# Loading q with four tokens to a partition in a fused retention and wave-MLP kernel

## The chip, the cores and the metric

The kernel runs on one core of one Trainium2 chip. The metric is the device time of one execution in microseconds. A core has five engines that run their own instruction lists in order and wait for one another by semaphores: TensorE (PE, with PEld for its weight loads), VectorE (DVE), ScalarE (ACT), GpSimd (POOL) and SyncE (SP). SP, ACT and POOL issue the DMAs; in this kernel SP and ACT issue the loads of q, k and v and the stores, SP also the transposes by DMA, POOL the loads of the weights.

## What is computed

Two layers follow one another. The first is a retention recurrence over 768 tokens, 4 batches and 8 heads of 64, the second a token- and channel-mixing layer over the 512 channels:

```python
for t in range(S):                       # q, k, v: (4, 8, 768, 64), float32
    state = gamma[h] * state + outer(k[t], v[t])
    y[t] = scale * q[t] @ state
x = y with the heads side by side        # (4, 768, 512)
theta = x @ w_theta
zr, zi = x * cos(theta), x * sin(theta)
u = x + w_tok_r @ zr + w_tok_i @ zi      # mixes tokens
out = u + relu(u @ w_ch)                 # (4, 768, 512), float32
```

gamma differs from head to head. The kernel writes the powers of gamma into q and v as factors that depend on the token's position (qsc, vsc), or into the result (qx), so that the recurrence becomes masked products of blocks.

## The kernel before

**Units.** The first layer is cut into 24 units: 4 batches, 3 blocks of 256 tokens, 2 halves of the heads. Unit n has 4 heads and 256 tokens. For each unit `Lk`, `Lq` and `Lv` load a tile of 128 partitions from k, q and v: partition p holds the tokens 2p and 2p+1 of all four heads, so a head gives a run of two tokens x 64 x 4 bytes, 512 bytes, and a load is one DMA of 512 such runs, 262144 bytes. `ck`, `cq`, `cqs` and `cv` turn the tiles into bfloat16 on POOL, DVE or ACT, `cqs` and `cv` with the position factors; the k and q halves land in one tile kqb.

**A unit's work.** `Tk` and `Tq` transpose kqb on PE and `E` copies the result to kqT (from unit 12 on `Dk` does both by DMA for some units). `A` makes the scores (L346), `m` multiplies them with the mask on DVE (L355), `Y` multiplies them with v (L423). `ST` makes the unit's contribution to the state, `S0` and `S1` sum it, `SB` writes it as a block diagonal, `I` multiplies it with q (L411). `XB` or `XA` evicts the result to xT, with heads and channels on the partitions and the tokens put back into their order. `Tx` and `Ex`, or `Dx` by DMA, transpose that into x_sb.

**The second layer.** A chunk is 128 tokens; two units (the two halves of heads) give two chunks. `Hh` makes the angles (L469), `CN` their cosine and sine on ACT (L476), `z` the products (L483). `M` mixes the tokens on PE (L509), `u` adds x, `Tu` and `Eu` or `Du` transpose, `O` multiplies with w_ch (L536), `f` finishes and `SO` stores.

**The order.** Nothing is scheduled by the compiler: ORDER is one list of tokens, each naming a function, its unit or chunk, and for copies and loads the engine (p, v, a, or s for SP). Each engine gets its instructions in the order of the list, so a token's place matters for its own engine. `Z` are warm-up matmuls on a tile of zeros: seven `Z` tokens with two matmuls each stand before `Tk.0`, seven more among the first units, one at the end. They wait for the memset of zero in `const1` on DVE, which stands behind the product arg in `const2`. `const2`, `constA`, `const4` and `const5` make the positions, the logarithms of gamma, the identity and the mask on POOL; ACT computes qsc and vsc in `const3` and the eight pieces of qx in `const8` and `const9` (L233), ahead of `ck.1.a`.

**The rotation of semaphores.** DMAs that SP and ACT issue (loads, stores, transposes) take eight completion semaphores in turn, in an order close to that of the list, whichever queue issues them. The issue of a DMA waits until the DMA that had its semaphore before has landed, and holds up what stands behind it on its queue. Before the change `Lv.4` so waits for `Lq.4`, and `Lk.5` for `Lk.4`. Tiles of the loads come from two pools, 16 for k and q, 9 for v.

Of the kernel before, what the change touches and what calls it, by code (L numbers as in the profile page):

```python
# [15 lines left out]
FT = mybir.dt.float32  # L16
# [7 lines left out]
const4 Lq.1.a const9 Lk.1.s Z.39 const8 ck.0.p Tk.0 ck.1.a cqs.0.v cv.0.v Tq.0 E.0.v Lq.4.a ST.0  # L24
Lk.4.a cqs.1.p Tq.1 Lq.2.s S0.0.v SB.0.1.v A.0 Lk.2.s SB.0.0.p cv.1.p Lv.2.s S1.0 Z.15 I.0 Z.27 m.0
Tk.1 E.1.a cqs.2.v Z.34 cv.2.p Y.0 ST.1 XB.0.1.a S0.1.v S1.1 SB.1.0.a Pth Lq.3.s Z.18 XB.0.0.v Tq.2
A.1 SB.1.1.a ck.2.a I.1 m.1 Y.1 ST.2 Tk.2 const7 Z.23 XB.1.0.v Lk.3.s E.2.v XB.1.1.v A.2 ck.3.p
S0.2.v m.2 S1.2 SB.2.1.a Z.11 cqs.3.p Tq.3 Lv.3.s Tx.0 Tk.3 Z.3 ck.4.p Lv.4.s Lk.5.s Lq.5.s Lv.5.s
Lq.6.s Lk.6.s Lv.6.s Lq.7.s E.3.a SB.2.0.v I.2 Y.2 XB.2.1.a Ex.0.a cv.3.v cq.4.p Tk.4 Lq.8.s A.3
ST.3 Lk.7.s S0.3.v SB.3.0.a S1.3 Lv.7.s Lk.8.s Tx.1 Tq.4 SB.3.1.p cv.4.p m.3 Pw.1.0 XB.2.0.a Ex.1.a  # L30
I.3 Lv.8.s E.4.a ck.5.a cq.5.a Y.3 Pw.0.0 ST.4 Hh.0 S0.4.v XB.3.0.v XB.3.1.v cv.5.v CN.0.1 A.4
CN.0.0 Tq.5 Hh.1 Tk.5 SB.4.0.p SB.4.1.a Pw.0.1 Hh.2 m.4 E.5.v I.4 Y.4 ST.5 ck.6.a Tk.6 Tx.2 cq.6.a
CN.1.1 CN.1.0 XA.4.1 A.5 XA.4.0 m.5 Lq.9.s Ex.2.v S0.5.v z.0.p Tq.6 E.6.a CN.2.0 cv.6.p Hh.3
SB.5.0.v Tx.3 Tw.1.0 z.1.v SB.5.1.a Ew.1.0.v Ex.3.a CN.2.1 A.6 I.5 Y.5 ST.6 XA.5.0 z.2.v Tw.0.0
CN.3.0 Tx.4 CN.3.1 Ew.0.0.v S0.6.v XA.5.1 Ex.4.v Hh.4 CN.4.0 CN.4.1 Tw.0.1 M.0.1 Pw.1.1 z.3.v M.0.0
Tw.0.2 Pw.1.2 Ew.0.2.a SB.6.1.a Hh.5 z.4.p SB.6.0.p Lk.9.a M.0.3 ck.7.p cqs.7.p M.0.2 CN.5.1 CN.5.0
cq.8.v m.6 Ew.0.1.v Tw.1.1 Tw.1.2 Ew.1.1.v Lv.9.s M.0.4 M.1.0 Tx.5 Ew.1.2.v M.1.1 S1.6 Tk.7 M.1.4
Pch Ex.5.v z.5.v cv.7.v Tq.8 Tq.7 M.1.2 E.7.a M.0.5 I.6 Y.6 ST.7 A.7 ck.8.a u.0 S0.7.v m.7 XA.6.1
SB.7.1.a M.1.5 M.1.3 XA.6.0 Tw.1.3 M.2.5 Pw.0.2 M.2.3 u.1 S1.7 Tk.8 M.2.1 M.2.0 SB.7.0.v Ew.1.3.a
Tu.0 I.7 cv.8.v E.8.a Lk.10.s ck.10.p cv.9.p Y.7 ST.8 A.8 cqs.9.v ck.9.v M.2.4 Du.1 Eu.0.a XB.7.1.a  # L40
# [6 lines left out]
Tu.3 Eu.3.a Dx.9 SB.10.0.a cqs.12.p u.4 Hh.9 Tq.11 ck.11.v Tu.4 z.6.v Eu.4.v ck.15.v M.5.0 M.5.4
Tk.11 E.11.a SB.10.1.p cv.11.p M.5.2 M.5.3 I.10 M.5.5 M.5.1 Lq.13.a A.11 Y.10 ck.14.v ST.11 CN.9.1
CN.9.0 SO.0.a Hh.8 u.5 S0.11.v z.9.v XB.10.0.v m.11 Dk.12 Tx.8 Tq.14 O.4 Lv.13.a SB.11.0.a Lq.15.s
Lk.13.s CN.8.1 Lk.18.a XB.10.1.a CN.8.0 SB.11.1.p cv.12.p Lq.16.s I.11 Tk.14 Ex.8.v A.12 Y.11 ST.12  # L50
f.4 Lv.15.s O.3 z.8.p E.14.a XA.11.0 XA.11.1 Hh.10 S0.12.a f.3 SB.12.0.v Tx.10 Tu.5 CN.10.1 Dx.11
Ex.10.v cq.13.p Lk.16.s Lv.17.s Hh.11 SO.2.s CN.10.0 m.12 S1.12 z.10.v Tk.15 M.6.1 M.6.2 M.6.0 M.6.3
# [12 lines left out]
S0.18.v XA.17.1 XA.17.0 O.10 SO.1.a CN.14.1 S1.18 Lv.19.a CN.14.0 Dx.16 Lq.20.a f.10 Lq.22.a
SB.18.0.a Hh.17 SB.18.1.p Eu.11.v Tq.19 I.18 Tk.19 CN.17.1 O.8 Tx.17 CN.17.0 m.18 Hh.16 z.14.p
Lv.20.s Du.9 E.19.a f.8 O.11 Y.18 cv.19.p ck.20.a CN.16.1 ST.19 A.19 CN.16.0 M.12.1 Ex.17.v f.11
cq.20.p Lk.22.s Dk.20 M.12.0 S0.19.a M.13.3 M.13.2 XB.18.1.a SB.19.1.p SB.19.0.v M.13.0 z.17.v
# [15 lines left out]
M.20.4 Mh.1.1 M.20.5 u.20 O.22 Mh.1.5 uh.1 f.22 Tu.20 SO.14.a SO.19.s Eu.20.a O.21 SO.18.a Tuh.1
Euh.1 f.21 Oa.0 Oa.1 fa.0 fa.1 Oh.0 Oh.1 SO.21.a SO.22.s SO.20.s fh.0 SOh.0 fh.1 SOh.1 Z.31
# [14 lines left out]
def kernel(  # L100
# [16 lines left out]
    P = 128  # L117
# [35 lines left out]

    def load_unit(name, src, n, e):
        b, i, h = unit(n)
        t = io.tile([P, HU, 2, D], FT, name="vf" if name == "vf" else "kqf", bufs=9 if name == "vf" else 16)
        queues[e].dma_start(  # L157
            out=t.rearrange("p h a d -> p h (a d)"),
            in_=src[b, h * HU:(h + 1) * HU, i * 2 * P:(i + 1) * 2 * P, :].rearrange(
                "h (p a) d -> p h (a d)", a=2))  # L160
        raw[name, n] = t
# [4 lines left out]
    def Lq(n, e):  # L166
        load_unit("qf", q, n, e)
# [35 lines left out]
    def const2():  # L203
        posn = const.tile([P, nI, 2], FT, name="posn")
        nc.gpsimd.iota(posn, pattern=[[2 * P, nI], [1, 2]], base=1, channel_multiplier=2,
                       allow_small_or_imprecise_dtypes=True)
        lg = const.tile([P, H], FT, name="lg")
# [11 lines left out]
        K["arg"] = arg  # L219

# [15 lines left out]
    def const3():  # L236
        K["qsc"] = const.tile([P, nI, 2, H], FT, name="qsc")
        K["vsc"] = const.tile([P, nI, 2, H], FT, name="vsc")
        for t, bias, sc in ((K["qsc"], K["lscale"], 1.0), (K["vsc"], K["zerob"], -1.0)):
            nc.scalar.activation(t.rearrange("p i a h -> p (i a) h"), K["arg"], AF.Exp,  # L240
                                 bias=bias, scale=sc)
        K["qx"] = const.tile([P, H // 2, S], FT, name="qx")
# [16 lines left out]
    def const5():  # L259
        mask = const.tile([P, 2, 2, D], BF, name="mask")  # L260
        nc.gpsimd.memset(mask, 1.0)
        for c in range(2):
            rows = slice(c * D, (c + 1) * D)
            for a in range(2):
                nc.gpsimd.affine_select(
                    out=mask[rows, a], in_=mask[rows, a], compare_op=ALU.is_ge, fill=0.0,
                    base=-a, pattern=[[1, 2], [2, D]], channel_multiplier=-2)
# [23 lines left out]
    def in_blocks(ap):  # L291
        return ap.rearrange("p (a h d) -> p a h d", a=2, h=HU)
# [4 lines left out]
    def cq(n, e):  # L297
        copy(e, in_blocks(kqb_of(n)[:, 1]), by_token(raw["qf", n]))
# [348 lines left out]
```

## Time and profile before

| | |
|---|---|
| time, median of 3 runs (lowest to highest) | 165.81 us (165.0 to 166.0) |
| span of the profiled execution, from its first to its last instruction | 163.6 us |
| PE busy | 155.2 us, 95%, 2034 matmuls |
| DVE, ACT, POOL busy | 114.0, 78.9, 74.3 us |
| DMA, mean rate over the span | 214 GB/s, 34.93 MB in 69062 packets |
| loads of q | 24 of 256 KB, 17 from SP and 7 from ACT |
| time of a q load from issue to landing, median | 5.8 us on SP, 5.2 us on ACT |

The page has only the span of the profiled execution; the 2.2 us between it and the median lie around the span. Busy time of an engine counts neither the issue of DMAs nor waiting. In a row of the timeline stand the start in us, the length in us, the engine, the line, the operation and its tiles, how many are merged (x8), and in brackets the idle time ahead of it with the work that ended it. "SPq" and "ACTq" rows are the queues' own work, above all DMA issues. In a row of groups stand the busy time, the mean of one in ns, and the idle time before.

### The profile page before, as it was taken

How to read it: one execution, taken by the hardware profiler on the slowest of the kernel's cores; microseconds unless marked ns; L12 is line 12 of the kernel's file. 1: busy time of each engine (PE TensorE's matmuls, PEld its weight loads, DVE VectorE, ACT ScalarE, POOL GpSimd, SP SyncE). 2: the span in 40 equal slices, each digit the busy share in tenths (PEclk: the TensorE clock that was granted, in tenths of full speed). 3: DMA queues.
4: the chain of work that ended last, by engine and by line, in shares of the span. 5: the costliest groups of instructions: out<-in, count | busy, mean ns of one | idle time of the engine just before them, and what ended most of it. 6: DMA issues, size and time to landing. Idle time of an engine off the chain costs nothing.

```text
span 163.6 us, 4928 instructions
## 1 busy us (share of the span) xinstructions
PE 155.2 (95%) x2034; PEld 87.2 (53%) x2034; DVE 114.0 (70%) x215; ACT 78.9 (48%) x140; POOL 74.3 (45%) x107
## 2 busy tenths in 40 slices
PE   5996889999999999999999999999999999999992
PEld 1453655656666655654554565554545554444561
DVE  3388687887994895984879894887867760345372
ACT  4976697974658255773343726732341616000020
POOL 7557389075034552730227599950469204600000
PEclk9999999999999999999999999999999999999999
DMA  3999999999999999999999999999897548515546
GB/s 115 297 290 255 268 283 236 275 220 286 220 162 232 223 291 139 338 203 270 324 263 198 134 268 221 242 193 298 125 245 136 103 92 227 160 64 128 129 164 224
DMA packets 69062, 34.93 MB, mean 214 GB/s; under 512 B 26416, under 2 KB 66096, under 8 KB 69040
## 3 DMA queue, kind: packets, MB, share of 16 engines
q1 hardware_dynamic: 56032, 23.73, 69.4%
q10 hardware_dynamic: 10320, 7.47, 17.7%
q0 software_dynamic: 2688, 3.41, 12.1%
q8 instruction: 16, 0.26, 0.7%
q14 instruction: 6, 0.05, 0.1%
HBM read 25.69 MB, written 6.29 MB: 196 GB/s over the span
## 4 chain that ended last, share of the span: by engine, by line
PE 76%; DMA 8%; ACT 5%; POOL 3%; issue 2%; SPq 2%; DVE 1%; POOLq 0%; ACTq 0%
PE y_ps L509 36%; PE o_ps L536 11%; PE th_ps L469 10%; DMA kqf<-in_k_dram 8%; PE r_ps L423 3%; ACT qx L233 3%; PE w_ps L491 3%; PE at_ps L346 3%; PE r_ps L411 2%; PE kq_ps L316 2%; SPq L157 2%; PE y_ps L561 2%; ACT cs L476 1%; PE x_ps L455 1%; PE r_ps L373 1%
## 5 line engine op out<-in xcount | busy, mean ns | idle before, releaser
L509 PE MATMUL y_ps<-z,wtr 128*128 128x512 bf16 x138 | 52.4, 380 | 0.0
L509 PE MATMUL y_ps<-z,wti 128*128 128x512 bf16 x138 | 52.3, 379 | 0.0
L483 POOL TENSOR_TENSOR z<-cs,x_sb 128x1024 bf16<-128x1024 bf16 x12 | 25.5, 2136 | 17.9 <-ACT cs L476 10.0
L355 DVE TENSOR_TENSOR at<-at_ps,mask 128x1024 bf16<-128x1024 f32 x24 | 29.2, 1216 | 0.2
L469 PE MATMUL th_ps<-wth,xT 128*128 128x512 bf16 x96 | 24.5, 379 | 0.5 <-ACT cs L476 0.4
L516 DVE TENSOR_TENSOR u<-y_ps,x_sb 128x512 bf16<-128x512 f32 x23 | 15.8, 688 | 12.7 <-PE y_ps L509 12.6
L542 DVE SCALAR_TENSOR_TENSOR ot<-o_ps,u 128x512 f32<-128x512 f32 x22 | 15.1, 688 | 12.5 <-PE o_ps L536 12.4
L308 POOL TENSOR_TENSOR vb<-vf,vsc 128x512 bf16<-128x512 f32 x15 | 15.6, 1041 | 17.3 <-DMA vf<-in_v_dram 16.9
L476 ACT ACTIVATE cs<-th_ps,zerob 128x512 bf16<-128x512 f32 x24 | 16.4, 685 | 13.3 <-PE th_ps L469 8.8
L536 PE MATMUL o_ps<-wch,uT 128*128 128x512 bf16 x88 | 22.6, 379 | 0.0
L476 ACT ACTIVATE cs<-th_ps,halfpi 128x512 bf16<-128x512 f32 x24 | 16.3, 686 | 11.5 <-issue 5.4
L509 PEld LDWEIGHTS <-wtr 128*128 128x128 bf16 x138 | 13.5, 98 | 12.7
L509 PEld LDWEIGHTS <-wti 128*128 128x128 bf16 x138 | 13.5, 98 | 12.0 <-issue 0.2
L139 POOL CAST sbd<-s 64x256 bf16<-64x256 f32 (+1 forms) x21 | 10.1, 481 | 20.8 <-DVE s L391 17.7
L137 ACT COPY kqT<-kq_ps 128x1024 bf16<-128x1024 bf16 x12 | 12.1, 1012 | 11.9 <-PE kq_ps L316 11.9
L469 PEld LDWEIGHTS <-xT 128*128 128x128 bf16 x96 | 8.8, 98 | 8.7 <-issue 0.5
L137 ACT CAST kqb<-kqf 128x512 bf16<-128x512 f32 x16 | 9.6, 620 | 6.9 <-DMA kqf<-in_k_dram 6.3
L536 PEld LDWEIGHTS <-uT 128*128 128x128 bf16 x88 | 8.1, 98 | 8.3
L278 PE MATMUL zz<-zero 128*128 128x512 bf16 x30 | 10.3, 476 | 1.9 <-DVE zero L192 1.9
L423 PE MATMUL r_ps<-at,vb 64*64 64x128 bf16 x384 | 9.9, 221 | 1.6 <-DVE at L355 1.6
L316 PE MATMUL kq_ps<-ident,kqb 128*128 128x128 bf16 x120 | 11.2, 220 | 0.3 <-POOL kqb L302 0.3
L139 POOL CAST kqb<-kqf 128x512 bf16<-128x512 f32 x12 | 7.2, 612 | 8.5 <-DMA kqf<-in_k_dram 8.4
(80 smaller groups left out, 208.7 us busy)
## 6 DMA issues: line engine op xcount, KB each, us to landing
vf<-in_v_dram SPq DMA_DIRECT2D x20, 256.0 KB, 5.9
kqf<-in_k_dram SPq DMA_DIRECT2D x19, 256.0 KB, 5.3
kqf<-in_q_dram SPq DMA_DIRECT2D x17, 256.0 KB, 5.8
out_dram<-ot ACTq DMA_DIRECT2D x12, 256.0 KB, 2.7
out_dram<-ot SPq DMA_DIRECT2D x11, 256.0 KB, 2.9
kqf<-in_q_dram ACTq DMA_DIRECT2D x7, 256.0 KB, 5.2
kqf<-in_k_dram ACTq DMA_DIRECT2D x5, 256.0 KB, 6.6
vf<-in_v_dram ACTq DMA_DIRECT2D x4, 256.0 KB, 5.8
```

The costliest lines, as they stand in the source:

```text
L137: nc.scalar.copy(dst, src)
L139: engines[e].tensor_copy(dst, src)
L308: engines[e].tensor_mul(in_blocks(vb), by_token(raw["vf", n]), _bcast_last(K["vsc"][:, i, :, h * HU:(h + 1) * HU], D))
L355: nc.vector.tensor_mul(at.rearrange("p g j a t -> p (g j) (a t)"), st["at_ps", n].rearrange("p g j a t -> p (g j) (a t)"), _bcast_mid(K["m ...
L423: nc.tensor.matmul(st["R", n + 1][c][g * D:(g + 1) * D, j * P:(j + 1) * P], st["vb", n][rows, lo:lo + D], st["at", n][rows, g, j, a, :], s ...
L469: nc.tensor.matmul(th_ps, st["xT", C][:, j, :], K["wth"][:, j, :], start=(j == 0), stop=(j == 3))
L476: nc.scalar.activation(st["cs", C][:, w, :], st["th_ps", C], AF.Sin, bias=K["zerob" if w else "halfpi"], scale=1.0)
L483: engines[e].tensor_mul(st["z", b][:, c], st["cs", C], _bcast_mid(x_of(C), 2))
L509: nc.tensor.matmul(st["y", t], K["wT"][r][:, s0, t0 * P:(t0 + 1) * P], st["z", b][:, s0, r, :], start=(done == 0 and r == 0), stop=(done = ...
L516: nc.vector.tensor_add(st["u", t], st["y", t], st["x", b][:, t0, :])
L536: nc.tensor.matmul(o_ps, st["uT", t][:, j, :], K["wch"][:, j, :], start=(j == 0), stop=(j == nD - 1))
L542: nc.vector.scalar_tensor_tensor(st["ot", t], st["o", t], 0.0, st["u", t], ALU.max, ALU.add)
```

## The change

A tile of q now has four tokens to a partition instead of two, and two heads instead of four: partition 64j + p holds the tokens 4p to 4p+3 of the heads 2j and 2j+1 of the unit. A head's run is 1024 bytes. Since a partition's two heads lie apart, a unit's q comes in two DMAs, one for g = 0 and one for g = 1, each with 128 runs, one to a partition, 131072 bytes. k and v are loaded as before.

What follows from it: the position factors of q need their own table (posq, lgq, argq, 2 iotas and 8 memsets of 64 partitions more on POOL, one product more on DVE); the columns of the transposed q stand in another order (`qT` picks 4 x 32 columns where 2 x 64 were taken), and with them the mask and the reordering of tokens in `XB` and `XA`. In ORDER `Lq.4.a` and `Lk.4.a` move from before `ST.0` to behind `Tk.1`, past unit 2's loads; all else keeps its order. No instruction of ACT stands between the two places.

```diff
 const4 Lq.1.a const9 Lk.1.s Z.39 const8 ck.0.p Tk.0 ck.1.a cqs.0.v cv.0.v Tq.0 E.0.v
-Lq.4.a ST.0 Lk.4.a cqs.1.p Tq.1 Lq.2.s S0.0.v SB.0.1.v A.0 Lk.2.s SB.0.0.p cv.1.p Lv.2.s S1.0 Z.15 I.0 Z.27 m.0 Tk.1 E.1.a
+ST.0 cqs.1.p Tq.1 Lq.2.s S0.0.v SB.0.1.v A.0 Lk.2.s SB.0.0.p cv.1.p Lv.2.s S1.0 Z.15 I.0 Z.27 m.0 Tk.1 Lq.4.a Lk.4.a E.1.a
...
     def Lq(n, e):
-        load_unit("qf", q, n, e)
+        b, i, h = unit(n)
+        t = io.tile([P, 2, 4, D], FT, name="kqf", bufs=16)
+        for g in range(2):
+            part = q[b, h * HU + g:h * HU + g + 1, i * 2 * P:i * 2 * P + 4, :]
+            queues[e].dma_start(
+                out=t[:, g].rearrange("p a d -> p (a d)"),
+                in_=bass.AP(tensor=part.tensor, offset=part.offset,
+                            ap=[[2 * S * D, 2], [4 * D, D], [1, 4 * D]]))
+        raw["qf", n] = t
...
+        posq = const.tile([P, nI, 4], FT, name="posq")
+        lgq = const.tile([P, H // 2], FT, name="lgq")
+        for j in range(2):
+            rows = slice(j * D, (j + 1) * D)
+            nc.gpsimd.iota(posq[rows], pattern=[[2 * P, nI], [1, 4]], base=1,
+                           channel_multiplier=4, allow_small_or_imprecise_dtypes=True)
+            for x in range(H // 2):
+                head = x // 2 * HU + 2 * j + x % 2
+                nc.gpsimd.memset(lgq[rows, x:x + 1], math.log(gammas[head]))
         lg = const.tile([P, H], FT, name="lg")
...
+        argq = const.tile([P, nI * 4, H // 2], FT, name="argq")
+        nc.vector.tensor_mul(argq, _bcast_last(posq.rearrange("p i a -> p (i a)"), H // 2),
+                             _bcast_mid(lgq, nI * 4))
...
-        mask = const.tile([P, 2, 2, D], BF, name="mask")
+        mask = const.tile([P, 2, 4, D // 2], BF, name="mask")
...
-                    base=-a, pattern=[[1, 2], [2, D]], channel_multiplier=-2)
+                    base=-a, pattern=[[1, 4], [4, D // 2]], channel_multiplier=-2)
...
+    def qT(n, rows, j, c):
+        lo = j * D + c * (D // 2)
+        return st["kqT", n][rows, 1, :, lo:lo + D // 2]
...
-                                         kqT[rows, 0, a, j, cols],
-                                         kqT[rows, 1, :, j, cols],
+                                         kqT[rows, 0, 2 * a + j, cols],
+                                         qT(n, rows, j, c),
...
-        return (st["xT", C][:, 2 * h:2 * h + 2].rearrange("p j (t a) -> p j t a", a=2),
-                st["R", n + 1][c][:, :2 * P].rearrange("p (j a t) -> p j t a", j=2, a=2))
+        return (st["xT", C][:, 2 * h:2 * h + 2].rearrange("p j (t a) -> p j t a", a=4),
+                st["R", n + 1][c][:, :2 * P].rearrange("p (j a t) -> p j t a", j=2, a=4))
```

More of the change, by code (lines that the diff above doesn't have):

```diff
@@ L35 @@
[L35 to L40, printed above, removed]
@@ L47 @@
[L47 to L52, printed above, removed]
@@ L65 @@
[L65 to L68, printed above, removed]
+const4 Lq.1.a const9 Lk.1.s Z.39 const8 ck.0.p Tk.0 ck.1.a cqs.0.v cv.0.v Tq.0 E.0.v ST.0 cqs.1.p Tq.1
+Lq.2.s S0.0.v SB.0.1.v A.0 Lk.2.s SB.0.0.p cv.1.p Lv.2.s S1.0 Z.15 I.0 Z.27 m.0 Tk.1 Lq.4.a Lk.4.a E.1.a
@@ new lines @@
+cqs.2.v Z.34 cv.2.p Y.0 ST.1 XB.0.1.a S0.1.v S1.1 SB.1.0.a Pth Lq.3.s Z.18 XB.0.0.v Tq.2 A.1 SB.1.1.a
+ck.2.a I.1 m.1 Y.1 ST.2 Tk.2 const7 Z.23 XB.1.0.v Lk.3.s E.2.v XB.1.1.v A.2 ck.3.p S0.2.v m.2 S1.2
+SB.2.1.a Z.11 cqs.3.p Tq.3 Lv.3.s Tx.0 Tk.3 Z.3 ck.4.p Lv.4.s Lk.5.s Lq.5.s Lv.5.s Lq.6.s Lk.6.s Lv.6.s
+Lq.7.s E.3.a SB.2.0.v I.2 Y.2 XB.2.1.a Ex.0.a cv.3.v cq.4.p Tk.4 Lq.8.s A.3 ST.3 Lk.7.s S0.3.v SB.3.0.a
+S1.3 Lv.7.s Lk.8.s Tx.1 Tq.4 SB.3.1.p cv.4.p m.3 Pw.1.0 XB.2.0.a Ex.1.a I.3 Lv.8.s E.4.a ck.5.a cq.5.a
@@ new lines @@
+Dx.9 SB.10.0.a cqs.12.p u.4 Hh.9 Tq.11 ck.11.v Tu.4 z.6.v Eu.4.v ck.15.v M.5.0 M.5.4 Tk.11 E.11.a
+SB.10.1.p cv.11.p M.5.2 M.5.3 I.10 M.5.5 M.5.1 Lq.13.a A.11 Y.10 ck.14.v ST.11 CN.9.1 CN.9.0 SO.0.a Hh.8
+u.5 S0.11.v z.9.v XB.10.0.v m.11 Dk.12 Tx.8 Tq.14 O.4 Lv.13.a SB.11.0.a Lq.15.s Lk.13.s CN.8.1 Lk.18.a
+XB.10.1.a CN.8.0 SB.11.1.p cv.12.p Lq.16.s I.11 Tk.14 Ex.8.v A.12 Y.11 ST.12 f.4 Lv.15.s O.3 z.8.p
+E.14.a XA.11.0 XA.11.1 Hh.10 S0.12.a f.3 SB.12.0.v Tx.10 Tu.5 CN.10.1 Dx.11 Ex.10.v cq.13.p Lk.16.s
@@ new lines @@
+Lv.17.s Hh.11 SO.2.s CN.10.0 m.12 S1.12 z.10.v Tk.15 M.6.1 M.6.2 M.6.0 M.6.3 CN.11.0 CN.11.1 M.7.3
+SB.12.1.a Lk.17.a ck.13.a M.7.4 M.7.0 M.6.4 Dk.13 M.7.1 z.11.v M.6.5 SO.3.s A.14 M.7.2 Eu.5.v I.12
+Lv.14.s u.6 cqs.15.v M.7.5 M.9.3 Tq.15 ck.17.a E.15.a m.14 SO.4.a Lq.17.s Lq.18.s Lk.21.s ck.16.a M.9.0
+M.9.5 M.9.1 M.9.4 Lq.19.a M.9.2 Du.6 cv.13.v u.7 M.8.0 u.9 Y.12 cv.14.p ST.13 A.13 O.5 XB.12.1.a
+XB.12.0.a M.8.1 S0.13.a S1.13 M.8.4 M.8.3 SB.13.0.a SB.13.1.p cq.16.p m.13 I.13 ck.18.a Y.13 ST.14 A.15
@@ new lines @@
+f.5 cq.17.v Lv.18.a M.8.5 M.8.2 XA.13.0 XA.13.1 S0.14.v SB.14.0.p Lv.16.s Hh.13 S1.14 u.8 Tx.12 M.10.1
+cv.15.p cv.17.p SB.14.1.p M.10.0 M.10.4 cqs.18.v M.10.5 CN.13.0 CN.13.1 Hh.12 CN.12.1 I.14 m.15 Y.14
+CN.12.0 ST.15 S0.15.v XB.14.1.a SB.15.0.a M.10.3 cv.16.v Dk.16 Dk.17 Du.7 Dx.13 M.10.2 Dk.18 O.6
+SB.15.1.p XB.14.0.v S1.15 I.15 Y.15 ST.16 SO.5.a cv.18.p f.6 S0.16.v A.16 M.11.4 SB.16.1.p M.11.1
+Lq.21.a Ex.12.a z.12.p SB.16.0.a Lk.19.s Lk.20.s XB.15.0.a u.10 z.13.p XB.15.1.a m.16 O.7 Du.10 I.16
@@ L219, in const2 @@
         K["arg"] = arg
+        argq = const.tile([P, nI * 4, H // 2], FT, name="argq")
+        nc.vector.tensor_mul(argq, _bcast_last(posq.rearrange("p i a -> p (i a)"), H // 2),
+                             _bcast_mid(lgq, nI * 4))
+        K["argq"] = argq
     def constA():
@@ L236, in const3 @@
     def const3():
-        K["qsc"] = const.tile([P, nI, 2, H], FT, name="qsc")
+        K["qsc"] = const.tile([P, nI, 4, H // 2], FT, name="qsc")
         K["vsc"] = const.tile([P, nI, 2, H], FT, name="vsc")
-        for t, bias, sc in ((K["qsc"], K["lscale"], 1.0), (K["vsc"], K["zerob"], -1.0)):
-            nc.scalar.activation(t.rearrange("p i a h -> p (i a) h"), K["arg"], AF.Exp,
+        for t, arg, bias, sc in ((K["qsc"], K["argq"], K["lscale"], 1.0),
+                                 (K["vsc"], K["arg"], K["zerob"], -1.0)):
+            nc.scalar.activation(t.rearrange("p i a h -> p (i a) h"), arg, AF.Exp,
                                  bias=bias, scale=sc)
@@ L325, in E @@
     def E(n, e):
-        kqT = work.tile([P, 2, 2, 2, P], BF, name="kqT", bufs=4)
-        copy(e, kqT.rearrange("p w a j t -> p (w a j) t"), st["kq_ps", n])
+        kqT = work.tile([P, 2, 4, P], BF, name="kqT", bufs=4)
+        copy(e, kqT.rearrange("p w x t -> p (w x) t"), st["kq_ps", n])
         st["kqT", n] = kqT
     def Dk(n):
-        kqT = work.tile([P, 2, 2, 2, P], BF, name="kqT", bufs=4)
+        kqT = work.tile([P, 2, 4, P], BF, name="kqT", bufs=4)
         nc.sync.dma_start_transpose(
-            out=kqT.rearrange("p w a j t -> p (w a j) t"),
+            out=kqT.rearrange("p w x t -> p (w x) t"),
             in_=st["kqb", n].rearrange("p w d -> p (w d)"))
         st["kqT", n] = kqT
+    def qT(n, rows, j, c):
+        lo = j * D + c * (D // 2)
+        return st["kqT", n][rows, 1, :, lo:lo + D // 2]
     def A(n):
@@ L411, in I @@
                 nc.tensor.matmul(r[c][:, j * P:(j + 1) * P], sbd_of(n)[:, c, j, :],
-                                 st["kqT", n][:, 1, :, j, c * D:(c + 1) * D],
+                                 qT(n, slice(0, P), j, c),
                                  start=(j == 0), stop=False, skip_group_check=True)
```

88 lines of the change are left out of this document (40 added, 48 removed).

## The prediction

> **What bounds the kernel now.** I read the page first (the span, the forty slices, the chain), then the waits of PE after the start, then the timeline of the first 28 us, and last the SP queue. All sums below are made in the profiled execution's own span of 163.6 us. The median of the runs shown is 165.81 us, 2.2 us above it, for what lies around the span; I add 2.2 to every sum.
>
> ```profile
> span 163.6 us, 4928 instructions
> ...
> PE   5996889999999999999999999999999999999992
> ...
> PE 76%; DMA 8%; ACT 5%; POOL 3%; issue 2%; SPq 2%; DVE 1%; POOLq 0%; ACTq 0%
> ```
>
> Each digit of the PE line is 4.09 us. From the eighth slice to the last but one TensorE is busy for nine tenths or more; only the first seven slices and the tail have room. How much room the middle has is told by the waits of PE between 27 and 164 us:
>
> ```profile
> PE th_ps L469 <- ACT cs L476: 0.4, 1, 0.4
> ```
>
> That is the whole answer: one wait of 0.4 us in 137 us. From 27.7 us on the kernel runs at TensorE's pace. A change to q's loads adds no matmul and removes none, so it can move the end only by moving the moment at which this stretch begins, or by tearing a hole into it. The gain is therefore small in any case; the loss isn't bounded in that way.
>
> What sets the beginning? In the first 27 us each unit n goes through a fixed ring: scores on PE (A.n, L346), the mask on DVE (m.n, L355), the value product on PE (Y.n, L423), then transposes and the scores of the next unit. From the timeline of all engines, unit 1:
>
> ```profile
> 12.12 0.42 PE L346 MATMUL at_ps<-kqT 64*64 64x128 bf16 x16
> ...
> 12.59 1.23 DVE L355 TENSOR_TENSOR at<-at_ps,mask 128x1024 bf16<-128x1024 f32 x1
> ...
> 13.86 0.42 PE L423 MATMUL r_ps<-at,vb 64*64 64x128 bf16 x16 [1.11 <-DVE at L355]
> ```
>
> PE stands still 1.11 us until the mask is done. Nothing in this ring waits for a load, so whatever delays its first turn delays all turns. It ends at the angle matmuls Hh.3, where two things meet; ACT first, PE below it:
>
> ```profile
> 25.37 1.14 ACT L137 CAST kqb<-kqf 128x512 bf16<-128x512 f32 x2 [0.85 <-DMA kqf<-in_k_dram]
> ```
>
> ```profile
> 26.94 0.40 PE L316 MATMUL kq_ps<-ident,kqb 128*128 128x128 bf16 x4
> 27.72 0.59 PE L469 MATMUL th_ps<-wth,xT 128*128 128x512 bf16 x2 [0.39 <-ACT cs L476]
> ```
>
> ACT waited 0.85 us for unit 6's k, then PE 0.39 us for ACT. So PE came to Hh.3 at 27.72 - 0.39 = 27.33 us: a ring that is late by up to 0.39 us costs nothing here, if the load comes earlier.
>
> **The change part by part.**
>
> *New constants (L219 to L223 and L238 of the changed file).* This is the part that I expect to be felt. GpSimd gets two iotas and eight memsets of 64 partitions ahead of the lg memsets; DVE gets argq behind arg. What hangs on them (GpSimd, DVE, PE, then the mask's two pairs in the chain and their group):
>
> ```profile
> 0.91 0.15 POOL L205 IOTA posn<- 128x6 f32 x1 [0.39 <-POOLq L631]
> 1.02 0.32 POOL L209 MEMSET lg<- 128x1 f32 x8
> ...
> 3.68 1.07 POOL L228 MEMSET lgp<- 64x1 f32 x8
> ```
>
> ```profile
> 1.38 0.21 DVE L217 TENSOR_TENSOR arg<-posn,lg 128x48 f32<-128x48 f32 x1 [1.38 <-POOL lscale L211]
> 1.59 0.27 DVE L192 MEMSET zero<- 128x256 uint32 x1
> ```
>
> ```profile
> 1.92 5.58 PE L278 MATMUL zz<-zero 128*128 128x512 bf16 x14 [1.92 <-DVE zero L192]
> 7.34 0.61 PE L316 MATMUL kq_ps<-ident,kqb 128*128 128x128 bf16 x8
> ```
>
> ```profile
> 1.76 0.54 POOL mask L265 x2
> 2.35 0.55 POOL mask L265 x2
> ```
>
> ```profile
> L265 POOL TENSOR_SCALAR_AFFINE_SELECT mask<-mask 64x128 bf16<-64x128 bf16 x4 | 1.1, 291 | 0.1
> ```
>
> lg goes to arg on DVE, behind arg stands the memset of zero, and on zero wait the 14 warm-up matmuls that PE works off in order before the first transpose at 7.34 us. So GpSimd's extra time goes, step for step, into the start of the ring. An iota of this kind takes 0.15 us, two 0.30. For the memsets there are two rows: eight of 128x1 took 0.32 us, 0.04 each; eight of 64x1, which go to the upper and the lower half in turn, took 1.07 us, 0.134 each. The new ones are 64x1 but stand four and four in one half. The mask's four instructions of 64 partitions, a pair to each half, tell the two apart: a pair takes 0.54 us, less than twice 0.291, so they overlap within a half; between the pairs (1.76 + 0.54 to 2.35) the engine is empty for 0.05. It is the change of half that costs. I take them nearer to the first row: 8 x 0.04 + 0.30 and some 0.1 for two changes of half, **0.7 us** (bounds 0.6 and 1.4). argq has the shape of arg, 0.21 us. Together PE's first matmul comes 0.9 us later (0.8 to 1.6).
>
> The same 0.7 us goes to ACT, whose decay table waits for lgp:
>
> ```profile
> 3.95 4.90 ACT L233 ACTIVATE qx<-pos,lscale,lgp 128x512 f32<-128x512 f32 x8 [0.43 <-POOL lgp L228]
> ```
>
> Behind it on ACT stand unit 1's k cast, then Lq.4 and Lk.4, which thus go out 0.7 us later, and one issue more of some 0.4 us ahead of Lk.4. The cast is late by less than PE is; this costs nothing beyond the 0.9. DVE has waited 3.26 us for q at 6.22 us, so argq costs nothing there.
>
> *q in 1024-byte rows.* The DMA's rate in a stretch with nothing but 512-byte loads, and that of a microsecond in which weight rows are loaded among them (windows; the last two columns are DMA share and GB/s):
>
> ```profile
> 8.00:12.00 4.00, 3.73 (x86) 2.25 (x82) 3.50 (x8) 2.91 (x6) 2.13 (x4) 1.00 1.22 290
> 19.00:20.00 1.00, 0.84 (x40) 0.73 (x28) 0.49 (x2) 0.73 (x2) 0.20 (x1) 1.00 1.16 347
> ```
>
> At 290 GB/s a load of 262144 bytes takes 0.90 us of DMA time, at 347 it would take 0.76. No row shows a 1024-byte load, so a q load saves between 0 and 0.15 us; by unit 6's k seven q loads stand ahead, 0 to 1.0 us. I take 0.1 each, 0.7 in all. It's worth only what the ring waits for loads: it takes away the 0.85 us wait of ACT, which the ring, 0.9 us late, takes away as well.
>
> *Two DMAs a unit, and the order of the semaphores.* DMAs from SP and ACT share eight semaphores in rotation: an issue waits until the eighth one before it has landed. The SP queue shows it, two v issues and then a k issue:
>
> ```profile
> 8.93 5.70 SPq L157 DMA_DIRECT2D vf<-in_v_dram  x2
> 15.94 0.37 SPq L157 DMA_DIRECT2D kqf<-in_k_dram  x1
> ```
>
> Unit 4's v waited for Lq.4, unit 5's k for Lk.4, both issued by ACT only after its table. In the changed order Lv.4 waits for Lv.2 and Lk.5 for the first half of Lq.4, both of which landed earlier than what they replace, or were issued before it. So they go out earlier; that too is worth only the 0.85 us wait. Moving the tokens Lq.4.a and Lk.4.a behind Lv.2.s does not move them on ACT (nothing of ACT stands between the old place and the new); it moves their place in the rotation, nothing else. SP and ACT pay one issue more for each q load, 17 on SP and 7 on ACT, about 0.5 us each. On ACT the tightest place has two q loads in a row:
>
> ```profile
> 101.17 0.52 ACTq L157 DMA_DIRECT2D kqf<-in_q_dram  x1
> 101.73 0.30 ACT L137 CAST sbd<-s 64x128 bf16<-64x128 f32 x1 [0.35 <-DVE s L139]
> 103.09 0.69 ACT L476 ACTIVATE cs<-th_ps,zerob 128x512 bf16<-128x512 f32 x1 [1.06 <-PE th_ps L469]
> ```
>
> Two more issues put that cast 1.0 us later; ACT then has 1.06 us of idle time ahead of its next piece. I cost it at nothing; if PE should wait for this cast, it would be up to 1 us.
>
> At 0.90 us of DMA time and 5.8 us to landing (the row stands below) several loads are under way at once, so a fixed cost of each is overlapped, and I count none. [...]
>
> *The views with four tokens instead of two (cq, cqs, A, I, XB, XA, mask).* Same instructions, partitions and elements, only other strides. XB and XA read PSUM in steps already; bounds 0 and a stretch that no row shows. I take nothing.
>
> **Sum.** Ring 0.9 us later, 0.39 swallowed at Hh.3: **+0.5 us**, 164.1 us of span, 166.3 us. With the bounds of the constants: +0.4 to +1.2, 166.2 to 167.0.
>
> **The rivals.**
>
> *The loads set the start.* The chain of waits gives DMA 8% of the span (the row above). If these pace the ring and not its own latency, the constants are hidden and the 0.85 us of ACT goes: 165.0 us. Against it: PE lost just 0.39 us to that chain.
>
> *The rotation holds back SP's transposes (the other side: slower).* The place is the stretch from 51 to 60 us, where SP goes from issue to issue and the transpose Dx.9 stands behind the loads; its tile is read by z.9 on DVE, ahead of all that DVE does later. The SP queue, the spread of these transposes' landing, z.9, and the time of a q load:
>
> ```profile
> 51.52 2.45 SPq L157 DMA_DIRECT2D kqf<-in_q_dram  x2
> ...
> 57.67 1.57 SPq L462 DMA_TRANSPOSE x_sb<-xT  x1
> ```
>
> ```profile
> DMA to landing us min/median/max: 2.4/4.1/6.3
> ```
>
> ```profile
> 65.66 0.68 DVE L483 TENSOR_TENSOR z<-cs,x_sb 128x1024 bf16<-128x1024 bf16 x1
> ```
>
> ```profile
> kqf<-in_q_dram SPq DMA_DIRECT2D x17, 256.0 KB, 5.8
> ```
>
> The list of work has four q loads on SP there (Lq.10, Lq.14, Lq.12, Lq.11): four more issues, 2.0 us. A load lands 5.8 us after its issue, eight issues at 0.5 are out after 4.0, so a wait of up to 1.8 us can come on top: 3.8 us. With the longest landing Dx.9's tile is there at 57.67 + 6.3 = 64.0, 1.7 us before z.9 at 65.66. From 1.7 us of delay DVE waits, and PE behind it; at 3.8 us it costs 2.1: +0.5 + 2.1, 168.4 us. For it: SP has hardly a gap there. Against it: cheaper rows shorten the queue, and the long issues look like pushback from it.
>
> *The wide rows bring nothing.* Then the rate stays at 290, and since it is hidden the time is the forecast's.
>
> **How the numbers follow.** Forecast 0.60 (166.2 to 167.0, the no-gain case in it), loads set the start 0.13 (165.0), rotation 0.22 (168.4), something unforeseen 0.05. The range goes from 165.0 to 168.4, from the one rival to the other. About 1% (1.7 us) is what a measurement of this kernel can tell from no change. Faster by that needs 164.1 or less, below every case: 0.04. Slower needs 167.5: the rotation, and part of the unforeseen: 0.25. Within 1%: 0.71.
>
> **What would show it.** Right: the first zz matmul near 2.8 instead of 1.92; Hh.3 near 28.2 with no wait of ACT for unit 6's k; Lk.5 out before 15.94; PE without waits after it. Wrong: new PE waits for kqT, x_sb or z between 50 and 90 us, or Hh.3 before 27.7 us.

## The result and the profile after

The changed kernel takes 270.92 us (median of 4 runs, 270.53 to 271.49), the kernel before beside it 165.61: a ratio of 1.64, with an interval of 1.633 to 1.642. The forecast was 166.3 us in a range from 165.0 to 168.4. It was wrong by 104.6 us. Executions over 1.5% longer than the fastest of the same kernel are left out of the times below, one of four in the experiment called four and two of four in that called eight, and the profiles of these two are of such executions.

The page of the kernel after: the span, PE by fortieths (6.75 us each), the clock granted to it, the share of the DMA engines, and the first line of the chain that ended last.

```profile
span 269.8 us, 4972 instructions
...
PE   5127505808909799606779199565929995899995
...
PEclk9957755975977979955959869967886999999999
DMA  3324382565669999448249953999999999745445
...
SPq 39%; DMA 24%; PE 24%; issue 4%; POOL 3%; ACT 2%; DVE 1%; POOLq 0%; DVEq 0%; ACTq 0%
```

Before, PE was busy from the eighth slice on and made up 76% of the chain. Now there are holes over the first three quarters, PE is 24% of the chain, and SP's queue together with DMA is 63%. One might read "waiting for DMA" as "too many bytes". The second and third slices say otherwise: PE is at 1 and 2 tenths there, and DMA at 3 and 2. Something waits for DMA while most of the DMA engines' time is idle. (In later holes of PE the DMA line stands higher, at 4 to 9, so the slices alone do not settle it.) Windows over the first stretch and one behind it show how idle (the columns behind the window: its length, busy time of PE, PE's weight loads, DVE, ACT and POOL, granted clock, DMA share, GB/s):

```profile
8.00:9.00 1.00, 0.00 (x0) 0.00 (x0) 0.00 (x0) 1.00 (x3) 0.00 (x0) 1.00 0.83 250
9.00:11.00 2.00, 0.00 (x0) 0.00 (x0) 0.00 (x0) 0.66 (x2) 0.00 (x0) 1.00 0.14 46
11.00:14.00 3.00, 0.00 (x0) 0.00 (x0) 0.19 (x1) 0.00 (x0) 0.00 (x0) 0.83 0.14 45
14.00:18.00 4.00, 1.03 (x20) 0.70 (x20) 2.50 (x6) 0.00 (x0) 0.00 (x0) 0.50 0.14 44
27.00:30.00 3.00, 0.68 (x18) 0.46 (x19) 1.16 (x2) 2.19 (x3) 0.07 (x1) 1.00 0.15 45
```

For nine microseconds on end, from 9 to 18, and again at 27, the share stands at 0.14 to 0.15 and the rate at 44 to 46 GB/s; before, a stretch with nothing but loads ran at a share of 1.22 and 290 GB/s. I read a level that is the same in every such stretch not as contention but as a fixed part of the engines at its full pace. 0.14 / 1.22 is 0.115, near two of the sixteen engines that the page's share refers to (0.125). At 45 GB/s one new q DMA of 131072 bytes takes 2.9 us and a unit's two take **5.8 us**, instead of the 0.90 us that a q load took.

SP's queue in the same stretch, and three rows of the list of waits:

```profile
6.93 7.21 SPq L171 DMA_DIRECT2D kqf<-in_q_dram  x2
14.18 4.12 SPq L157 DMA_DIRECT2D kqf<-in_k_dram  x1
```

```profile
POOL vb L330 <- DMA vf<-in_v_dram: 40.6, 5, 15.8
ACT kqb L135 <- DMA kqf<-in_k_dram: 28.8, 6, 8.6
...
DVE kqb L324 <- DMA kqf<-in_q_dram: 23.4, 4, 10.0
```

The issue of two q DMAs holds SP for 7.21 us, and the longest of these waits are for v and k, whose loads were not changed. (All waits of the list for q together are 77 us, for k 70, for v 49.) My reading is that the loads of k and v are spread over all engines, and land only when the two that are full of q have got to their share; no view lists the engines of a single load.

The pattern is in the diff: the source of the new DMA is `[[2 * S * D, 2], [4 * D, D], [1, 4 * D]]`, with the two heads as its outermost count. The destination has 128 there, as source and destination of every load of q, k and v had before. That the source's 2 is what holds a load to two of the page's sixteen engines is my reading: it fits the share of 0.14, no row of this profile shows it, and the experiments test it.

### The profile page after: what moved, and what is told of

Read it like the earlier page. It is cut to its first block, busy times and chain, and to the rows that moved or that the text cites. A ratio compares the mean times of both kernels' runs of the same rounds, so it can differ in the third digit from the quotient of the medians.

```text
span 269.8 us, 4972 instructions
## 1 busy us (share of the span) xinstructions
PE 182.7 (68%) x2034; PEld 98.6 (37%) x2034; DVE 114.4 (42%) x216; ACT 79.3 (29%) x140; POOL 75.1 (28%) x117
## 3 DMA queue, kind: packets, MB, share of 16 engines
HBM read 25.69 MB, written 6.29 MB: 119 GB/s over the span
## 4 chain that ended last, share of the span: by engine, by line
SPq 39%; DMA 24%; PE 24%; issue 4%; POOL 3%; ACT 2%; DVE 1%; POOLq 0%; DVEq 0%; ACTq 0%
SPq L157 18%; SPq L171 18%; DMA kqf<-in_q_dram 16%; PE y_ps L535 9%; PE o_ps L562 6%; DMA x_sb<-xT 6%; PE th_ps L495 4%; DMA uT<-u 3%; SPq L354 2%; POOL z L509 2%; ACT cs L502 1%; SPq L488 1%; PE r_ps L449 1%; PE y_ps L587 1%; POOL vb L330 1%
## 5 line engine op out<-in xcount | busy, mean ns | idle before, releaser
L535 PE MATMUL y_ps<-z,wtr 128*128 128x512 bf16 x138 | 56.2, 407 | 5.8 <-DVE z L509 5.8
L535 PE MATMUL y_ps<-z,wti 128*128 128x512 bf16 x138 | 55.9, 405 | 0.0
L338 PE MATMUL kq_ps<-ident,kqb 128*128 128x128 bf16 x120 | 15.2, 270 | 40.3 <-ACT kqb L135 19.1
L562 PE MATMUL o_ps<-wch,uT 128*128 128x512 bf16 x88 | 26.9, 435 | 11.1 <-ACT sbd L135 5.7
L338 PEld LDWEIGHTS <-kqb 128*128 128x128 bf16 x120 | 10.7, 122 | 46.9 <-ACT kqb L135 19.7
L495 PE MATMUL th_ps<-wth,xT 128*128 128x512 bf16 x96 | 27.8, 418 | 0.1
L535 PEld LDWEIGHTS <-wti 128*128 128x128 bf16 x138 | 14.3, 103 | 18.8 <-issue 7.6
L137 POOL CAST sbd<-s 64x256 bf16<-64x256 f32 (+1 forms) x21 | 9.3, 445 | 35.7 <-DVE s L417 28.2
L437 PE MATMUL r_ps<-kqT,sbd 128*128 128x128 bf16 x80 | 10.1, 249 | 9.6 <-issue 7.1
L324 DVE TENSOR_TENSOR kqb<-kqf,qsc 128x512 bf16<-128x512 f32 x6 | 4.1, 688 | 23.4 <-DMA kqf<-in_q_dram 23.4
```

The source lines that it names most:

```text
L137: engines[e].tensor_copy(dst, src)
L338: nc.tensor.transpose(st["kq_ps", n][:, 4 * w + x, :], st["kqb", n][:, w, x * P:(x + 1) * P], K["ident"])
L495: nc.tensor.matmul(th_ps, st["xT", C][:, j, :], K["wth"][:, j, :], start=(j == 0), stop=(j == 3))
L535: nc.tensor.matmul(st["y", t], K["wT"][r][:, s0, t0 * P:(t0 + 1) * P], st["z", b][:, s0, r, :], start=(done == 0 and r == 0), stop=(done = ...
L562: nc.tensor.matmul(o_ps, st["uT", t][:, j, :], K["wch"][:, j, :], start=(j == 0), stop=(j == nD - 1))
```

## The experiments

**Theory A**: the outermost count of 2 puts each q load on two engines, and all else waits for these. The rivals that the profile after leaves standing: rows of 1024 bytes are slow by themselves; or twice as many DMAs, in another order through the eight semaphores, choke the queues.

*Halves of the partitions.* As the changed kernel, but each of the two DMAs fills 64 partitions with both heads, tokens outermost:

```
- out=t[:, g].rearrange("p a d -> p (a d)"),     ap=[[2*S*D, 2], [4*D, D], [1, 4*D]]
+ out=t[j*D:(j+1)*D].rearrange("p g a d -> p g (a d)"), ap=[[4*D, D], [S*D, 2], [1, 4*D]]
```

> The changed kernel, but each of the two DMAs of a q load fills 64 partitions with both heads instead of 128 partitions with one head: the source is then walked by 64 groups of tokens first, not by 2 heads. Same 1024-byte rows, 128 rows and 128 KB a DMA, the same 48 DMAs, tables, views and ORDER. Theory A (a DMA is spread over as many DMA engines as the outermost count of its source allows, so the changed kernel's q loads ran on 2 of 16): the loads are back on 16 engines, no stretch at 45 GB/s is left, 165 to 167.5 us; the warm-up begins 0.85 us late as in the changed kernel and the rest of the step is the forecast's +0.5. Rival B (48 DMAs instead of 24 in a rotation of eight semaphores hold back the queues) and rival C (1024-byte rows at this distance are slow to read): nothing of theirs is changed, so about 270 us.

Measured: 170.42 us (170.31 to 170.75), ratio 1.029 [1.026, 1.032]. A hundred microseconds are gone with rows, number of DMAs, order, tables and views as in the changed kernel. It is 2.9 us above the upper end of what theory A expected of it. Windows of this run:

```profile
8.00:9.00 1.00, 1.00 (x16) 0.60 (x18) 0.00 (x0) 1.00 (x3) 0.36 (x1) 1.00 1.20 274
9.00:10.00 1.00, 0.52 (x21) 0.38 (x20) 0.91 (x3) 1.00 (x3) 0.68 (x1) 1.00 1.16 224
```

From 9 to 10 us, with halves of q under way, the rate is 224 GB/s with the engines nearly as busy as before (1.16 and 1.22 to 1.23); before, it was 290 to 291. Over the four microseconds from 8 to 12 it is 265 GB/s at 1.19, against 290 at 1.22 before, though not in every microsecond (296 GB/s from 10.5 to 11.5). I take it that a DMA that writes 64 partitions is slower even at the full share; why, no run shows, and other loads are under way in the same microseconds.

*Two DMAs with the old rows.* The kernel before, with q in two DMAs of two heads each (512-byte rows, partitions outermost) and the changed order of the work:

```
+ for g in range(2):
+     dma_start(out=t[:, 2*g:2*g+2], in_=<heads 2g, 2g+1 of the unit, "h (p a) d -> p h (a d)">)
```

> The kernel before with its 512-byte rows, but each q load in two DMAs of two heads each (128 partitions by 2 heads by 512 bytes, source walked by 128 partitions first), and the changed ORDER. Theory A: 16 engines, 165 to 167 us. Rival B: 48 DMAs and the rotation are all there, so most of the 105 us come back, 230 us or more. Rival C: rows as before, so as before.

Measured: 166.11 us (165.46 to 166.47, 10 runs), ratio 1.0026 [1.0009, 1.0042]. Twice as many DMAs and the rotation cost 0.4 us, and that rival falls. Nor does the trace show the 0.4 us as a price of each DMA. Unit 1's q now comes to POOL at 7.08 us instead of 7.34, so that POOL and DVE multiply at the same time; DVE's product vb takes 1.53 us instead of 0.69 (the mean of all nine is 774 ns instead of 682), PE waits 1.05 us for it, and unit 6's scores start 0.40 us late (29.67 instead of 29.27). Behind them PE waits for nothing more.

*How much of it, and where.* Two runs with the changed kernel's form for some units only, and halves for the others. First for every other unit:

```
+ if n % 2 == 1: <the changed kernel's two DMAs>   (second run: if n == 9)
+ else:          <the two halves>
```

> The changed kernel with q loads as changed for the 12 units of odd number, and as in e1_halves for the other 12. Theory A, from the changed kernel's 45 GB/s while only q loads ran (131072 bytes in 2.9 us): 24 DMAs x 2.9 = 70 us on the two engines, where 48 took 140; what else these two engines carry was about 110 us by the kernel before's rates, so 180 to 205 us. Rival B: as many DMAs, about 270. Rival C: as many 1024-byte rows, about 270.

Measured: 223.0 us, ratio 1.347 [1.342, 1.353]. That is above the expected 180 to 205: I had added up what the two engines carry, as if they were never without work. Then for unit 9 alone:

> Only unit 9's q load as changed, all others as in e1_halves. Theory A: its two DMAs keep two engines for 5.8 us longer than the rest; loads behind it land up to 5.8 us late, which the work in stock at that point hides in part: 0 to 5 us over e1_halves. Rivals B and C: about 270 us.

Measured: 174.9 us (173.82 and 175.98), ratio 1.056 [1.047, 1.064]. One unit costs 4.5 us over the halves (3.4 and 5.6 in the two runs); twelve cost (223.0 - 170.4) / 12 = 4.4 each; all twenty-four (270.9 - 170.4) / 24 = 4.2 each. So the cost is near linear at 1, 12 and 24 units. Two engines' 5.8 us for a unit's q replace some 1.2 us (262144 bytes at the 224 GB/s above), and little of the difference is hidden. With unit 9 alone the longest wait of PE behind the start, 3.0 us, is for vb, made from a load of v that was not changed.

*The count alone.* In the changed kernel the two outer entries of the source pattern change places, and nothing else:

```
- ap=[[2 * S * D, 2], [4 * D, D], [1, 4 * D]]
+ ap=[[4 * D, D], [2 * S * D, 2], [1, 4 * D]]
```

> Only the two outer entries of the source pattern change places (64 groups of tokens outermost, 2 heads inside): the same bytes, the same 1024-byte rows, two loads a unit over 128 partitions. A partition then holds another head and token than the tables assume, so q is computed with the wrong rows; the work is the same. Theory A (the outermost count of a load sets how many of the 16 DMA engines carry it, 2 in the changed kernel): all 16 carry it, no stretch with a share of 0.14 is left, 165.6 to 167.5 us. With it the rest of the halves' run is told apart: if its 4.8 us over the kernel before came from loads that write 64 partitions each, they are gone here; if they came from 1024-byte rows or from the four-token views, this run stays at 169.5 to 171. If neither holds and wide rows or two loads are the cause after all: about 270 us.

Measured: 167.01 us (165.87 to 167.56), ratio 1.008 [1.005, 1.011]. **104 us hang on the order of two entries in one pattern.** (This kernel computes q from the wrong rows; it is a test and no version to use.) Rows of 1024 bytes fall as a cause too, and of the halves' 4.8 us over the kernel before 3.4 are gone. The two runs differ only in which rows a load brings to which partitions, 64 or 128 of them. A microsecond with loads of q under way, and four microseconds around it, in this run:

```profile
10.50:11.50 1.00, 0.95 (x10) 0.64 (x10) 1.00 (x2) 0.00 (x0) 0.98 (x2) 1.00 1.06 317
8.00:12.00 4.00, 3.80 (x66) 2.18 (x69) 2.87 (x6) 2.59 (x6) 3.01 (x4) 1.00 1.07 293
```

317 GB/s at a share of 1.06; the same microsecond before ran at 291 and 1.23:

```profile
10.50:11.50 1.00, 1.00 (x36) 0.54 (x34) 0.71 (x3) 0.94 (x1) 0.00 (x0) 1.00 1.23 291
```

In such a microsecond the wider rows are the faster ones. Over the four microseconds, however, the rate is 293 GB/s against the 290 before: the engines are occupied less (1.07 against 1.22), and no more bytes come in.

*Four and eight.* If theory A is right, the cost must follow the count. Two runs read the same bytes in the same rows by as many DMAs over 128 partitions, but from 4 heads and from 8:

```
+ ap=[[S * D, 4], [4 * D, P // 4], [1, 4 * D]]      (four)
+ ap=[[S * D, 8], [4 * D, P // 8], [1, 4 * D]]      (eight)
```

> As the changed kernel, but each of the two loads of a unit takes 32 rows of four tokens from 4 heads (count 4 outermost) instead of 64 rows from 2. Bytes, row length, partitions and number of loads are the same; heads and tokens land in other partitions than the tables assume, so q is computed with the wrong rows. Theory A: four engines, so where q moves alone the share is near 4/16 = 0.27 and the rate near 90 GB/s, a unit's q takes 2.9 us of these engines instead of 5.8, that is 2.0 over the 0.9 of a load on all; times 24 at most 48 us: 175 to 215 us. Rival (two is a special case, any other count is spread on all engines): 165.6 to 170.5 us. Rival (any pattern with the heads outermost is equally slow): about 270 us.

> The same with 16 rows from each of 8 heads (count 8 outermost); q is computed with the wrong rows. Theory A: eight engines, share near 0.55 and 180 GB/s where q moves alone, 1.5 us a unit, 0.6 over 0.9; times 24 at most 14 us: 166.5 to 180 us. Rival (two and four are slow for another reason than the number of engines, and eight is spread on all): 165.6 to 166.5 us.

Measured: 208.2 us, ratio 1.257 [1.253, 1.262], and 177.9 us, ratio 1.074 [1.071, 1.078]; both kernels compute q from the wrong rows. (Four of sixteen is 0.25, not the 0.27 expected.) Stretches at the lowest level, which I read as q moving alone, the first row of the run with four, the second of that with eight:

```profile
8.00:10.00 2.00, 0.77 (x7) 0.33 (x5) 0.63 (x2) 1.66 (x4) 0.00 (x0) 1.00 0.28 88
```

```profile
11.00:12.00 1.00, 0.00 (x0) 0.00 (x0) 0.00 (x0) 0.00 (x0) 0.82 (x1) 1.00 0.55 170
```

Shares of 0.14, 0.28, 0.55 and rates of 45, 88, 170 GB/s: each doubling of the count doubles both.

| outermost count | GB/s | a unit's q, us | time, us | us a unit over the next row |
|---|---|---|---|---|
| 2 | 45 | 5.8 | 270.9 | 2.6 for 2.8 us of q |
| 4 | 88 | 3.0 | 208.2 | 1.3 for 1.4 |
| 8 | 170 | 1.5 | 177.9 | 0.5 for 0.7 |
| 64 (share 1.06) | 317 | 0.8 | 167.0 | |

(262144 bytes by the rate; the last column is the difference of the times by 24 units, and the difference of the column before it.) Theory A holds, with the engines read off the share: of each microsecond that a unit's q is longer, 0.6 to 0.9 reaches the end. (With the 293 GB/s of four microseconds the last row has 0.9 us, and the one above it 0.5 for 0.6.)

*The constants alone.* What is left, 167.0 against 165.65, should be my step for the new constants, +0.5. The kernel before with posq, lgq and argq at their places, read by nothing:

```
+ posq, lgq: two iotas and eight memsets ahead of lg      (GpSimd)
+ argq = posq * lgq, behind arg                           (DVE)
```

> The kernel before with the new constants alone (posq, lgq, argq at their places; nothing reads them, everything else as before). My recorded step: first zz matmul 0.9 us later, 0.39 of it swallowed at the angle matmuls, +0.5 us: 165.9 to 166.6 us, first zz at 2.6 to 2.8 us. Rival (loads pace the start and hide the constants): 165.4 to 165.7 us, with the zz as late.

Measured: 166.99 us (166.71 to 168.25), ratio 1.0092 [1.0064, 1.0120]: +1.34, as much as the run with the entries swapped has in all, and above what I expected. The cause is in the first ten microseconds. Before (ACT's queue, POOL, PE; the first instruction is unit 1's q):

```profile
1.76 0.44 ACTq L157 DMA_DIRECT2D kqf<-in_q_dram  x1
...
7.34 1.08 POOL L302 TENSOR_TENSOR kqb<-kqf,qsc 128x512 bf16<-128x512 f32 x1 [1.40 <-DMA kqf<-in_q_dram]
...
8.80 0.42 PE L346 MATMUL at_ps<-kqT 64*64 64x128 bf16 x16
```

With the constants alone:

```profile
2.40 1.28 ACT L253 ACT_TABLE_LOAD   x1 [2.40 <-DVE arg L226]
2.49 0.41 ACTq L157 DMA_DIRECT2D kqf<-in_q_dram  x1
2.77 4.74 PE L291 MATMUL zz<-zero 128*128 128x512 bf16 x14 [2.77 <-DVE zero L192]
...
7.35 0.61 PE L329 MATMUL kq_ps<-ident,kqb 128*128 128x128 bf16 x8
...
8.43 1.04 POOL L315 TENSOR_TENSOR kqb<-kqf,qsc 128x512 bf16<-128x512 f32 x1 [1.23 <-DMA kqf<-in_q_dram]
...
9.53 0.40 PE L329 MATMUL kq_ps<-ident,kqb 128*128 128x128 bf16 x4 [1.32 <-POOL kqb L315]
...
9.86 0.42 PE L359 MATMUL at_ps<-kqT 64*64 64x128 bf16 x16
```

ACT's table load waits for arg, and the issue of unit 1's q stands behind it. It goes out 0.73 us later, behind SP's next loads; POOL gets its q 1.09 us later, and PE's first scores are 1.06 late. The late zero costs nothing here: the warm-ups begin 0.85 us later, yet the first transposes stand at 7.35 us, where they were (7.34). PE then waits 1.32 us for POOL's product, 0.27 before. So it is the late load that starts the ring late.

The counter-test puts the same constants behind const3 in the order, past zero and past that issue:

```
- const2 (with posq, lgq, argq) ... const1 ... const5 ... const3 ...
+ const2 ... const1 ... const5 ... const3 const2b (posq, lgq, argq) ...
```

> The kernel before with the new constants, but behind const3 in the order, so that GpSimd makes them after the mask and DVE makes argq after zero and the state buffers; nothing reads them. Theory (the constants cost what they hold up at the head of three queues: the memset of zero on DVE, and ACT's table load with the issue of unit 1's q behind it, 2.49 us instead of 1.76): zz at 1.92 and that issue at 1.76 again, lgp and the decay table on ACT still 0.7 us late, which ACT's 1.09 us of idle time ahead of kqT hides: 165.5 to 166.0 us. Rival (what costs is the later decay table on ACT, or the work itself): 166.7 to 167.3 us as with the constants in front.

Measured: 165.48 us (165.22 to 166.31, 12 runs), ratio 0.9998 [0.9983, 1.0012]. The work itself costs nothing; its place cost 1.3 us. (This run takes zero and the issue of q out of the way together; that it is the issue is told by the rows above.)

*Both together.* The entries swapped, and the constants late as in the last run; the exponential of q's table goes behind `Lq.1.a`:

```
- ... const3 ... const4 Lq.1.a const9 ...
+ ... const3 const2b ... const4 Lq.1.a const2c (qsc = exp(argq + lscale)) const9 ...
```

> The run with the two outer entries swapped, with the constants made behind const3 and the exponential of q's table issued behind unit 1's q; q is computed with the wrong rows, as there. If the 1.36 us of that run were the constants' alone and q in 1024-byte rows by two loads on all 16 engines is worth nothing: 165.5 to 166.1 us. If the wide rows save loading time that the constants ate: below 165.4 us. If two loads a unit cost 0.45 us on top: 166.1 to 166.6 us.

Measured: 166.82 us (166.42 to 167.28), ratio 1.007 [1.005, 1.010]: a miss, 0.7 above what I expected for constants out of the way and 0.2 above the case in which two loads cost something on top. The trace shows where most of the 1.27 us arises. The first piece is at unit 0:

```profile
6.80 1.34 POOL L328 TENSOR_TENSOR kqb<-kqf,qsc 128x512 bf16<-128x512 f32 x1
7.17 1.53 DVE L334 TENSOR_TENSOR vb<-vf,vsc 128x512 bf16<-128x512 f32 x1
...
8.75 0.32 PE L403 MATMUL r_ps<-vb,kqb 64*64 64x64 bf16 x16 [0.69 <-DVE vb L334]
...
9.36 0.42 PE L376 MATMUL at_ps<-kqT 64*64 64x128 bf16 x16
```

q now comes early enough for POOL and DVE to multiply at the same time, and DVE's takes 1.53 us instead of the 0.69 it took in the kernel before, where it began 0.5 us ahead of POOL's:

```profile
6.83 0.69 DVE L308 TENSOR_TENSOR vb<-vf,vsc 128x512 bf16<-128x512 f32 x1
```

PE waits 0.69 us for it, and its first scores start at 9.36 us instead of 8.80. It is what the run with two DMAs and the old rows had (9.38), so its 0.4 us are no second piece beside this one. Unit 6's scores are 0.58 us late (29.85 instead of 29.27). Behind them stands a wait that neither that run nor the kernel before has, for a transpose by DMA, at 102.95 us:

```profile
PE o_ps L566 <- DMA uT<-u: 0.5, 1, 0.5
```

What is left stays open (0.2 us of the medians' 1.27, 0.5 us of the 1.6 between the two spans). For the change it means: with q at a share of 1.05 (291 GB/s from 8 to 12 us) and the constants out of the way it is no faster than the kernel before, so no version that beats it came out of these runs.

## Why the prediction was wrong

- **The step that failed** is *q in 1024-byte rows*: "a q load saves between 0 and 0.15 us ... I take 0.1 each". I costed the load by its row length, with the rate of loads whose pattern has 128 partitions outermost, and did not ask on how many engines the new pattern is spread. Instead of 0.8 us a unit it is 5.8, at the share of 0.14 that I read as two engines, and since the loads of k and v wait behind it, the kernel is over 4 us longer for each unit. The bounds had no loss in them: I let wide rows bring between nothing and something. With the two entries swapped the term lies within its bounds (0.07 us a load by 317 for 291 GB/s, 0.01 by 293 for 290).
- *Two DMAs a unit, at nothing*: 0.4 us measured, with the DMAs at the full share (1.22 and 290 GB/s from 8 to 12 us, as before), by two products that run at the same time at the start; a fixed cost of each DMA does not show. I weighed the number of the DMAs and overlooked their pattern, which decides: 270.92 us as they are, 167.01 with two entries swapped.
- *Constants*: the first zz matmul came at 2.77 us, near 2.8 as worked out, but the step's worth was 1.34 us, not 0.5. I let the late zero go "step for step, into the start of the ring"; the first transposes came when they had come before. And I said of ACT that its delay "costs nothing beyond the 0.9", looking only at what stands behind the decay table. The issue of unit 1's q stands ahead of it, behind the table load. Hh.3 did swallow its part and more: unit 5's scores start 1.30 us late, Hh.3 0.75 (28.47 instead of 27.72), without a wait for ACT. But the transposes behind it now wait 0.24 us for ACT, and unit 6's scores are 1.12 us late again. The rows before and with the constants alone:

```profile
26.59 0.42 PE L346 MATMUL at_ps<-kqT 64*64 64x128 bf16 x16
...
29.27 0.42 PE L346 MATMUL at_ps<-kqT 64*64 64x128 bf16 x16
```

```profile
27.89 0.42 PE L359 MATMUL at_ps<-kqT 64*64 64x128 bf16 x16
...
28.47 1.03 PE L482 MATMUL th_ps<-wth,xT 128*128 128x512 bf16 x3
29.73 0.38 PE L468 MATMUL x_ps<-ident,xT 128*128 128x128 bf16 x4 [0.24 <-ACT kqT L137]
...
30.39 0.42 PE L359 MATMUL at_ps<-kqT 64*64 64x128 bf16 x16
```

- *The views, at nothing*: nothing that these runs can see. The run with the entries swapped has the views and the wide rows and takes 167.01, the constants alone 166.99.
- *What bounds the kernel*: PE from 27.7 us on was a right reading of the kernel before, and its remark that the loss isn't bounded held. It gave a wrong sense of safety: one wait of 0.4 us in 137 says that loads came in time, not by how much. (The 2.2 us added to each sum are in part a difference between executions: in every run that lists both, 1.7 to 1.8 us lie between its time and its span.)
- *The rivals*: that issues hold back SP's queue did happen (7.21 us for one pair), but from 7 us on and not first at 51 to 60; whether such an issue waits for its semaphore or for the two full engines is not told apart here. The rival in which the loads set the start had the right object and the wrong sign. None had a load that becomes many times slower.

## What to carry to other kernels

Read the access pattern of a changed DMA from the outside in before costing its bytes: an outermost count of 2 moved 45 GB/s here where 64 or 128 moved 265 to 293, and other loads waited behind it. A low, level DMA share (0.14, 0.28, 0.55 with counts of 2, 4 and 8) in stretches in which all wait for DMA was the mark of it; look for it in windows of a few microseconds, since long slices average it away. A load that comes earlier can cost too, when it makes two engines work at once (DVE's product took 1.53 us beside POOL's here, instead of 0.69). Constants at the head of a queue cost what stands behind them, the issues of the first loads above all (1.34 us here); the same constants a few places later cost nothing here (165.48 us against 165.55).

## What the runs showed of the hardware that was not expected

- A q load at a share of 0.14 (two engines, as I read it) lengthens the kernel by most of its own extra time: 4.2 to 4.5 us for each unit's q, near linear in the number of such units, with 16 buffers for k and q to load ahead into.
- A microsecond with DMAs into 64 partitions ran at 224 GB/s, one with DMAs into 128 at 290, at nearly the same share of busy engines (1.16 and 1.22); over four microseconds it was 265 and 290 (1.19 and 1.22).
- DVE's 128x512 multiply took 1.53 us when POOL's had begun 0.37 us ahead of it (6.80 and 7.17), 0.69 when it began 0.51 ahead of POOL's (6.83 and 7.34, the kernel before). DVE's ended at 8.70, 0.56 us after POOL's (8.14): most of the 0.69 us that it takes otherwise stands behind POOL's end. Why, no run shows. In the same run DVE's product before that began 0.51 us ahead of POOL's (6.29 and 6.80) and took 0.95.
- PE's holes cost more than their length: the granted clock falls to 0.83 and 0.50 in them (11 to 14 and 14 to 18 us), PE's busy time goes from 155.2 to 182.7 us for the same 2034 matmuls, and the 138 of one group take longer on the mean, 407 ns where the run with halves has 380, first the kernel after:

```profile
L535 PE MATMUL y_ps<-z,wtr 128*128 128x512 bf16 x138 | 56.2, 407 | 5.8 <-DVE z L509 5.8
```

```profile
L535 PE MATMUL y_ps<-z,wtr 128*128 128x512 bf16 x138 | 52.4, 380 | 0.0
```
